# The value products of a pair of heads in one visit of the tensor engine instead of two

## The chip, the cores and the metric

The kernel runs on one core of a Trainium2 chip. The metric is the device time of one execution in microseconds (us). Engines are named as the profile names them: PE is the tensor engine (matmuls; PEld its weight loads), DVE the vector engine, ACT the scalar engine, POOL the GpSimd engine, SP the queue that issues the transfers.

## The reference

Attention with a decay, then a soft mixture of experts, then a second, dense mixture. The change touches the attention alone, which for 4 batches x 8 heads of 576 positions and 64 channels is

```python
scores = scale * np.matmul(q, k.transpose(0, 1, 3, 2))
cum = np.cumsum(log_f, axis=-1)
decay = cum[:, :, :, None] - cum[:, :, None, :]
scores = np.where(causal, -1000000000.0, scores + decay)
scores = scores - np.max(scores, axis=-1, keepdims=True)
attn = np.exp(scores)
attn = attn / (np.sum(attn, axis=-1, keepdims=True) + 1e-09)
return np.matmul(attn, v).astype(np.float32)
```

The two mixtures behind it (some 460 of the 674 us of the profile) work on its output and are the same in both kernels.

## The kernel before

The 32 heads run as 16 pairs. The 576 rows of a head are cut into row blocks j = 0 to 3 of 128 rows and j = 4 of 64 rows; being causal, block j needs keys up to its own end only. A pair takes seven steps, `STEPS`: head 0 with blocks 0 and 1 together (step 0), 3 (step 1) and 2 (step 2); block 4 of both heads at once (step 3); head 1 with blocks 0 and 1 (step 4), 3 (step 5) and 2 (step 6). I call S0 to S6 the scores of these steps and T0 to T6 their transposes.

- **Scores, `scores(g)`.** Each product is two matmuls in float32r (lines 227 and 228); step 3 is eight matmuls on line 212 into two PSUM tiles `sc`. Then `soft` runs: a DVE instruction on line 198 adds the mask and finds the row minimum while it moves the scores into the buffer `p` of that block, and ACT takes the exponential in place (line 202, followed by its read of the row sum, which gives the signal that the block is ready). There is one `p` buffer for each block number. For step 3 DVE does this in two pieces (384 and 192 columns), then ACT takes all 576 columns in one instruction, and two small DVE copies on line 219 (`rs<-r`) take the row sums from what ACT left.
- **Transposes, `transposes(g)`.** PE turns each 128x128 piece of `p` into a PSUM tile `pt` (lines 249, 251, 258; two such tiles in turn), and DVE or ACT copies it to SBUF, into `pta` (blocks 0 and 1) or `ptb` (blocks 2, 3, 4), by line 170 (DVE), 168 (ACT) or 255. They run two steps behind the scores.
- **Value products.** `av_a` (line 288) multiplies `pta` and `av_b` (line 276) `ptb` by v, for the pair before the one whose scores are running. Both heads' products go to the two halves of the partitions of one PSUM tile, with 64 columns of weights each, as two matmuls side by side. `av_b(pr, i, q0, q1)` takes key block i and query columns q0 to q1 of the 320 that `ptb` holds: columns 0 to 127 are row block 2, 128 to 255 row block 3, 256 to 319 row block 4. After i = 2 the tile is copied to `ot` by ACT and the next v is loaded (`load_v`).
- **Operands of the next pair.** `split_a` and `split_b` cast and split q and k into `opd`: for the next pair's head 0 at steps 3 and 4, which must wait until S3 has read the old one. That is a cast on ACT (line 168), one on DVE (line 170, 128x576), a copy and two subtractions on POOL (lines 180, 179 and 190).

**Order.** In the attention PE runs in the order in which the code stands (`manual_schedule` with PE alone); DVE, ACT, POOL and SP are put in order by the framework. At step st of a pair the loop issues S(st), then `before_tr`, then T(st-2), then `after_tr`. So PE's order is: S2, **visit 1**, T0, S3, **visit 2**, T1, S4, T2, S5, T3, `nat` (line 303), S6, `plog` (lines 322 and 324), T4, S0 and T5, S1 and T6, S2 of the next pair. Visit 1 holds `av_a` and three calls of `av_b`, visit 2 the other three. Every fourth pair has the batch's own work as well (`dlog`, `csoft1`, `dnat`, `sadd`).

Of the kernel before, what the change touches and what calls it, by code (L numbers as in the profile page):

```python
# [34 lines left out]
def soft_moe_kernel(tc, a, out):  # L35
# [12 lines left out]
    with ExitStack() as top:  # L48
# [117 lines left out]
        def copy(eng, o, i):  # L166
            if eng is act:
                act.copy(o, i)  # L168
            else:
                dve.tensor_copy(o, i)  # L170
# [98 lines left out]
        def av_b(pr, i, q0, q1=320):  # L269
            if i == 3:  # L270
                av[pr] = tlq.tile([128, 512], F32, tag="av", name=f"avb_{pr}")
            t = av[pr]
            kk = 64 if i == 4 else 128
            b0 = 960 if i == 4 else 320 * i + q0
            for hh in range(2):
                pe.matmul(t[64 * hh:64 * hh + 64, q0:q1], lhsT=v_raw[pr][:kk, i, 64 * hh:64 * hh + 64],  # L276
                          rhs=ptb[2 * pr + hh][:kk, b0:b0 + q1 - q0], start=i == 3, stop=i == 2, skip_group_check=True)
            if i == 2:
                copy(EV[7], ot[pr][:, 256:576], t[:, 0:320])
                if pr + 1 < B * NP:  # L280
                    load_v(pr + 1)

        def av_a(pr, i):
            if i == 0:
                av[pr] = tlq.tile([128, 512], F32, tag="av", name=f"ava_{pr}")
            t = av[pr]
            for hh in range(2):
                pe.matmul(t[64 * hh:64 * hh + 64, 128 * i:256], lhsT=v_raw[pr][:, i, 64 * hh:64 * hh + 64],  # L288
                          rhs=pta[2 * pr + hh][:, 256 * i:256 + 128 * i], start=i == 0, stop=i == 1)
            if i < 1:  # L290
                return
            ot[pr] = ot_t
            copy(EV[0], ot[pr][:, 0:256], t[:, 0:256])
            ri = sm.tile([128, 5, 2], F32, tag="ri", bufs=2, name=f"ri_{pr}")
            h0 = 2 * pr % 6
            dve.tensor_scalar(ri, rs[:, :, h0:h0 + 2], 1e-9, None, op0=ALU.add)
            dve.reciprocal(ri, ri)
            rinv[pr] = ri
# [14 lines left out]
        def nat(pr):  # L313
            b, p = divmod(pr, NP)
            if p == 0:
                xn[b] = xnp.tile([128, 5, DM], F32, tag="xn", name=f"xn_{b}")
            nat_dve(pr, nat_pe(pr))
# [83 lines left out]
        def sadd(b, between=None):  # L401
            dn = lb[b]["dn"]
            t = tlq.tile([128, 512], F32, tag="av", name=f"sa_{b}")
            for c in range(4):
                o = 32 * c
                pe.matmul(t[o:o + 32, :], lhsT=dn[:, c, :], rhs=xn[b][:, c, :], start=True, stop=False)
            if between:
                between()
            for c in range(4):
                o = 32 * c  # L410
                n = slice(128 * c, 128 * c + 128)
                pe.matmul(t[o:o + 32, n], lhsT=dn[:64, 4, :], rhs=xn[b][:64, 4, n], start=False, stop=True)
            if b == B - 1:
                return t
            dve.scalar_tensor_tensor(s_sb, s_sb, lb[b]["al"], t, op0=ALU.mult, op1=ALU.add)
# [3 lines left out]
        def logits(pr):  # L419
            b, p = divmod(pr, NP)  # L420
            plog(pr)
            if p == NP - 1:
                rep4(b)

        def before_tr(g):

            pr, st = divmod(g, NS)
            pr -= 1
            if pr < 0:
                return  # L430
            b, p = divmod(pr, NP)
            if st in (2, 3):
                if st == 2:
                    for i in range(2):
                        av_a(pr, i)

                for x in ((3, 128), (4, 256), (0, 128)) if st == 2 else ((0, 0, 128), (1, 0), (2, 0)):
                    av_b(pr, *x)
            elif st == 6 and b and p == 0:
                sadd(b - 1)  # L440
                nat(pr)
            elif st == 6 and pr < LASTP:
                logits(pr)
# [49 lines left out]
        for g in range(NG + 4):  # L493
            pr, st = divmod(g, NS)
# [29 lines left out]
            if g == NG:  # L524
                load_pair("opd1")
            before_tr(g - LAG + 2)
            if LAG <= g < NG + LAG:
                transposes(g - LAG)
# [16 lines left out]
        pr = B * NP - 1  # L545
        with tc.manual_schedule(engines={E.PE, E.Activation, E.DVE}):
# [49 lines left out]
            i4t, st, dg, one = scr[0:32, 0:128], scr[0:32, 128:130], scr[0:32, 130:162], scr[0:32, 162:290]  # L596
# [490 lines left out]
        with tc.manual_schedule(engines={E.PE, E.Activation, E.DVE, E.Pool}):  # L1087
            for m in range(NM):
# [82 lines left out]
                if e == E2 - 1:  # L1171
                    for tt in range(2):
                        i = 2 * nb + tt
# [59 lines left out]
```

## Time and profile before

| what | number |
|---|---|
| time, median of 3 runs | 677.42 us (676.77 to 678.02) |
| the profiled execution | 675.4 us, of which 673.6 us are its span |
| PE busy over the span | 657.5 us, 98% |
| DVE / ACT / POOL busy over the span | 494.5 / 341.8 / 419.0 us |
| from 100 to 140 us (attention): PE / DVE / ACT / POOL busy, of 40 us | 39.92 / 34.41 / 27.40 / 26.81 us |
| value products of line 276 | 384 matmul instructions, 43.8 us busy |

The attention runs from the start to about 212 us. Each float32 matmul of the code shows as two instructions in the trace. A matmul's row tells when it started and a modelled time until its result stands, so rows of one engine overlap; how long PE really spends on something is read from one start to the next. The span leaves out 1.8 us around it that the time has.

### The profile page before, as it was taken

The page shows a single profiled execution, that of the slowest core. Times are in us where ns is not written, and L with a number is a line of the kernel's source. Part 1 is how long each engine was busy: PE and PEld are TensorE (multiplying, and loading weights), DVE is VectorE, ACT ScalarE, POOL GpSimd, SP SyncE. Part 2 cuts the span into 40 slices and gives each one's busy share as a digit, 9 for nine tenths or more (in the row PEclk, how much of TensorE's full clock was granted, in tenths as well). Part 3 has the DMA queues.
Part 4 walks back from the last instruction along what each step waited for, and adds up shares of the span by engine and source line. Part 5 has one row for each costly group of instructions (what it writes and reads, how often), then busy time and mean ns, then how long its engine had stood idle before and what let it go on. Part 6 is the DMA issues. An engine that isn't in the chain of part 4 may idle for free.

```text
span 673.6 us, 15304 instructions
## 1 busy us (share of the span) xinstructions
PE 657.5 (98%) x5642; PEld 580.3 (86%) x5642; DVE 494.5 (73%) x1358; ACT 341.8 (51%) x817; POOL 419.0 (62%) x392
## 2 busy tenths in 40 slices
PE   5999999999999998999999999999999999999997
PEld 3877777777777446999999999999999999999997
DVE  7888988988986103976778876778876778877774
ACT  4776767767763015543446443446543356543441
POOL 5677767767751046944589844589934589935442
PEclk7999999999999999999999999999999999999999
DMA  6678788733318894033000303000303000011111
GB/s 184 189 261 254 220 279 262 229 93 117 93 55 310 334 419 165 2 126 126 1 1 2 126 1 125 2 1 2 124 3 111 15 1 1 32 37 59 48 48 63
DMA packets 27138, 76.15 MB, mean 113 GB/s; under 512 B 3772, under 2 KB 4156, under 8 KB 27064
## 3 DMA queue, kind: packets, MB, share of 16 engines
q1 hardware_dynamic: 27064, 75.18, 32.5%
q8 instruction: 45, 0.74, 0.5%
q14 instruction: 29, 0.24, 0.1%
HBM read 70.31 MB, written 4.72 MB: 111 GB/s over the span
## 4 chain that ended last, share of the span: by engine, by line
PE 91%; DVE 3%; ACT 2%; issue 2%; SPq 1%; DMA 1%; POOL 0%; ACTq 0%; DVEq 0%
PE R L1023 27%; PE Q L1023 13%; PE P L1023 6%; PE avb L276 6%; PE pt L258 5%; PE two L835 5%; PE sc L228 3%; PE d L1043 3%; PE sc L212 3%; PE sc L227 3%; PE two L731 2%; PE pl L324 2%; PE pt L249 2%; PE ava L288 2%; PE so_ps L755 2%
## 5 line engine op out<-in xcount | busy, mean ns | idle before, releaser
L901 POOL TENSOR_TENSOR s<-S,s 128x512 fp32r<-128x512 f32 x136 | 174.9, 1320 | 134.7 <-ACT s L897 134.7
L897 ACT CAST s<-S 128x512 fp32r<-128x512 f32 x136 | 75.0, 619 | 85.9 <-DVE S L893 47.9
L202 ACT ACTIVATE p<-p,nm 128x256 f32<-128x256 f32 (+2 forms) x144 | 83.4, 580 | 37.7 <-DVE nm L198 36.9
L1023 PE MATMUL R<-wh_T,s 128*128 128x256 f32 x544 | 86.6, 281 | 0.7 <-DVE acc L1006 0.7
L1006 DVE SCALAR_TENSOR_TENSOR acc<-R,dpn,acc 128x256 f32<-128x256 f32 x115 | 55.4, 482 | 37.2 <-PE R L1023 34.2
L867 ACT ACTIVATE a<-two 128x256 f32<-128x256 f32 x68 | 26.1, 384 | 96.9 <-PE two L835 90.5
L1023 PEld LDWEIGHTS R<-wh_T,s 128*128 128x128 f32 x544 | 73.4, 188 | 1.4 <-ACT a L876 1.2
L198 DVE CUSTOM_DVE_ANT_0 p<-sc,maskb 128x256 f32<-128x256 f32 (+2 forms) x144 | 66.1, 488 | 3.3 <-PE sc L212 0.9
L893 DVE SCALAR_TENSOR_TENSOR S<-two,S 128x256 f32<-128x256 f32 x136 | 57.0, 419 | 3.4 <-POOL s L901 0.8
L893 DVE SCALAR_TENSOR_TENSOR S<-two,a 128x256 f32<-128x256 f32 x136 | 56.2, 413 | 0.0
L179 POOL TENSOR_TENSOR opd<-raw,opd 64x576 fp32r<-64x576 f32 x30 | 44.6, 1487 | 11.2 <-ACT opd L168 9.8
L258 PE MATMUL pt<-ident,p 128*128 128x128 f32 x288 | 47.3, 283 | 1.8 <-DVE ptb L255 0.8
L227 PE MATMUL sc<-opd 128*128 128x256 f32 (+3 forms) x128 | 47.1, 378 | 1.6 <-ACT opd L168 1.6
L190 POOL TENSOR_TENSOR opd<-raw,opd 64x576 fp32r<-64x576 f32 x31 | 44.1, 1424 | 6.7 <-DVE opd L170 5.7
L258 PEld LDWEIGHTS pt<-ident,p 128*128 128x128 f32 x288 | 31.3, 142 | 17.6 <-issue 13.1
L835 PE MATMUL two<-c4t,gs 128*128 128x256 f32 x288 | 46.1, 283 | 0.3 <-ACT gs L168 0.3
L883 DVE SCALAR_TENSOR_TENSOR q<-two,q 128x512 fp32r<-128x512 f32 x68 | 46.2, 679 | 0.0
L1023 PE MATMUL R<-wh_T,q 128*128 128x256 f32 x272 | 43.8, 283 | 0.0
L276 PE MATMUL avb<-ptb,v 128*64 128x192 f32 (+3 forms) x384 | 43.8, 347 | 0.0
L1023 PE MATMUL Q<-wh_B,s 128*128 128x256 f32 x272 | 43.2, 281 | 0.0
L1023 PE MATMUL Q<-wh_T,s 128*128 128x256 f32 x272 | 43.1, 280 | 0.0
L1023 PE MATMUL R<-wh_B,a 128*128 128x256 f32 x272 | 43.0, 280 | 0.0
(244 smaller groups left out, 1662.5 us busy)
## 6 DMA issues: line engine op xcount, KB each, us to landing
w<-in_w SPq DMA_DIRECT2D x50, 512.0 KB, 4.9
ring<-in_m SPq DMA_DIRECT2D x28, 512.0 KB, 6.2
raw<-in_k SPq DMA_DIRECT2D x64, 144.0 KB, 2.8
v<-in_v SPq DMA_DIRECT2D x16, 320.0 KB, 4.0
out<-acc SPq DMA_DIRECT2D x18, 256.0 KB, 2.0
raw<-in_q SPq DMA_DIRECT2D x15, 288.0 KB, 4.3
ring<-in_w SPq DMA_DIRECT2D x8, 512.0 KB, 4.7
w_opd<-in_w SPq DMA_DIRECT2D x4, 512.0 KB, 6.0
```

Source lines behind the costliest of these rows:

```text
L198: dve.tensor_tensor_reduce(out=pt_in[j][:, k0:k0 + n], in0=sc, in1=maskb[:, m0:m0 + n], scale=-SCALE, scalar=nm, op0=ALU.add, op1=ALU.min, ...
L202: act.activation(p, p, AF.Exp, bias=nm, scale=-1.0, accum_out=sums)
L227: pe.matmul(o, lhsT=qa[hh][:, qs], rhs=ka[hh][:, 0:n], start=True, stop=False)
L258: pe.transpose(t[:, i, :], pt_in[j][:, 128 * i:128 * i + 128], ident)
L276: pe.matmul(t[64 * hh:64 * hh + 64, q0:q1], lhsT=v_raw[pr][:kk, i, 64 * hh:64 * hh + 64], rhs=ptb[2 * pr + hh][:kk, b0:b0 + q1 - q0], star ...
L835: pe.matmul(t[:, j, k], lhsT=gs[e][:, 128 * fc:128 * fc + 128], rhs=c4t[:, nb * BLK:nb * BLK + BLK])
L883: dve.scalar_tensor_tensor(o[:, 1], i, 0.0, f32(o[:, 0]), op0=ALU.max, op1=ALU.subtract)
L893: dve.scalar_tensor_tensor(sv[m, name][:, c], half[m, h][:, :, k, 128 * t:128 * t + 128], 0.0, other, op0=ALU.max, op1=op)
L897: act.copy(tile_of(m, name)[:, 0], sv[m, name])
L901: (eng or pool).tensor_tensor(o[:, 1], sv[m, name], f32(o[:, 0]), op=ALU.subtract)
L1006: dve.scalar_tensor_tensor(o, t, pcol, o, op0=ALU.mult, op1=ALU.add)
L1023: pe.matmul(t, lhsT=a[:, c, :], rhs=w[:, c, :], start=first and x == 0 and c == 0, stop=x == 2 and c == 3, skip_group_check=True)
```

## The change

In `before_tr` the second visit goes, and its three calls of `av_b` follow the first visit's. The call (1, 0), key block 1 with all 320 columns, is cut in two, (1, 128) and (1, 0, 128), so that everything which needs only columns from 128 on stands first, and the calls with columns 0 to 127, which need T6 of head 1, stand last.

```diff
-            if st in (2, 3):
-                if st == 2:
-                    for i in range(2):
-                        av_a(pr, i)
-
-                for x in ((3, 128), (4, 256), (0, 128)) if st == 2 else ((0, 0, 128), (1, 0), (2, 0)):
+            if st == 2:
+                for i in range(2):
+                    av_a(pr, i)
+                for x in ((3, 128), (4, 256), (0, 128), (1, 128), (0, 0, 128), (1, 0, 128), (2, 0)):
                     av_b(pr, *x)
```

PE in the kernel before, the end of visit 1 in the fourth pair, up to the beginning of visit 2 (L276 are the value products, L249 is T0, L212 is S3; in brackets what a row waits for):

```order
L276 MATMUL avb_682<-ptb_553,v_550 64x192
L276 MATMUL avb_682<-ptb_588,v_550 64x192
L249 MATMUL pt_689<-ident,p_122 128x128 [waits PE_49,Activation_49]
L249 MATMUL pt_689<-ident,p_123 128x128 x2
L212 MATMUL sc_0_695<-opd_92 128x384 [waits Pool_49]
L212 MATMUL sc_0_695<-opd_91 64x384 x2
L212 MATMUL sc_0_695<-opd_92 128x384 [waits DMAHW3_49,Pool_49]
L212 MATMUL sc_1_696<-opd_92 128x192
L212 MATMUL sc_1_696<-opd_91 64x192 x2
L212 MATMUL sc_1_696<-opd_92 128x192
L276 MATMUL avb_682<-ptb_553,v_550 64x128
L276 MATMUL avb_682<-ptb_588,v_550 64x128 [waits Activation_49]
```

The same place on PE in the changed kernel, from the new (1, 128) on:

```order
L276 MATMUL avb_686<-ptb_592,v_526 64x192
L276 MATMUL avb_686<-ptb_557,v_526 64x128
L276 MATMUL avb_686<-ptb_592,v_526 64x128 [waits Activation_49]
L276 MATMUL avb_686<-ptb_557,v_526 64x128
L276 MATMUL avb_686<-ptb_592,v_526 64x128
L276 MATMUL avb_686<-ptb_557,v_526 64x320
L276 MATMUL avb_686<-ptb_592,v_526 64x320
L249 MATMUL pt_704<-ident,p_122 128x128 [waits PE_49]
L249 MATMUL pt_704<-ident,p_123 128x128 x2
L212 MATMUL sc_0_710<-opd_92 128x384 [waits Pool_49]
L212 MATMUL sc_0_710<-opd_91 64x384 x2
L212 MATMUL sc_0_710<-opd_92 128x384 [waits DMAHW3_49,Pool_49]
```

All value products now stand ahead of T0 and S3, and T1 (line 258) follows right behind the last row of S3. S3 waits for POOL and a transfer as before.

DVE before, at the same place: the two pieces of S3 (line 198, tile `sc_0` and `sc_1`), the cast of the next pair's k between them, and what follows:

```order
L198 ISA p_126,nm_4_0_706<-sc_0_695,maskb 128x384 [waits PE_49,Activation_49]
L198 ISA nm_4_0_706 128x1
L170 CAST opd_91<-raw 128x576 [waits DMAHW1_49,DMAHW7_49,PE_49,Pool_49]
L198 ISA p_126,nm_4_1_708<-sc_1_696,maskb,nm_4_0_706 128x192 [waits DVE_49,PE_49]
L198 ISA nm_4_1_708 128x1
L219 COPY rs<-r_3_705 64x1 [waits Activation_49]
L219 COPY rs<-r_3_705 64x1
L170 COPY ptb_727<-pt_726 128x4x128 [waits PE_49]
L198 ISA p_123,nm_1_0_738<-sc_733,maskb 128x256 [waits PE_49]
```

And in the changed kernel:

```order
L198 ISA p_126,nm_4_0_721<-sc_0_710,maskb 128x384 [waits PE_49,Activation_49]
L198 ISA nm_4_0_721 128x1
L170 CAST opd_91<-raw 128x576 [waits DMAHW1_49,DMAHW2_49,PE_49,Pool_49]
L198 ISA p_126,nm_4_1_723<-sc_1_711,maskb,nm_4_0_721 128x192 [waits DVE_49,PE_49]
L198 ISA nm_4_1_723 128x1
L170 COPY ptb_733<-pt_732 128x4x128 [waits PE_49]
L198 ISA p_123,nm_1_0_744<-sc_739,maskb 128x256 [waits PE_49,Activation_49]
L198 ISA nm_1_0_744 128x1
L219 COPY rs<-r_3_720 64x1 [waits Activation_49]
L219 COPY rs<-r_3_720 64x1
```

The cast still stands between the two pieces; the copy of T1's result and the first piece of S4 have moved ahead of the two small copies that wait for ACT.

## Rows read from the trace of the kernel before

**Rows 1.** Busy time of each engine, granted clock, DMA share: a stretch of attention.
```profile
100.00:140.00 40.00, 39.92 (x331) 30.38 (x331) 34.41 (x127) 27.40 (x81) 26.81 (x31) 1.00 0.74 227
```

**Rows 2.** Timeline of PE over one pair (start us, us, what): S3 to S3.
```profile
99.82 1.31 PE L212 MATMUL sc<-opd 128*128 128x384 f32 x8
...
104.48 0.63 PE L258 MATMUL pt<-ident,p 128*128 128x128 f32 x4
...
107.66 0.28 PE L228 MATMUL sc<-opd 66*128 66x128 f32 x1
107.78 0.62 PE L258 MATMUL pt<-ident,p 128*128 128x128 f32 x4
...
108.74 0.52 PE L258 MATMUL pt<-ident,p 128*128 128x128 f32 x3
...
111.71 1.33 PE L212 MATMUL sc<-opd 128*128 128x384 f32 x8
```

**Rows 3.** Timeline of PE in short windows of the next pair: the value products.
```profile
110.13 0.28 PE L288 MATMUL ava<-pta,v 128*64 128x128 f32 x2
110.24 0.49 PE L276 MATMUL avb<-ptb,v 128*64 128x192 f32 x4
...
112.77 0.27 PE L212 MATMUL sc<-opd 66*128 66x192 f32 x1
...
112.97 0.71 PE L276 MATMUL avb<-ptb,v 128*64 128x128 f32 x6
...
113.24 0.71 PE L276 MATMUL avb<-ptb,v 128*64 128x320 f32 x4
...
114.04 0.44 PE L276 MATMUL avb<-ptb,v 128*64 128x320 f32 x2
114.41 0.33 PE L258 MATMUL pt<-ident,p 128*128 128x128 f32 x1
...
116.20 0.63 PE L258 MATMUL pt<-ident,p 128*128 128x128 f32 x4
```

**Rows 4.** Timeline of DVE, ACT and POOL behind S3 of the first pair.
```profile
100.91 0.56 DVE L198 CUSTOM_DVE_ANT_0 p<-sc,maskb 128x384 f32<-128x384 f32 x1
...
101.12 0.67 POOL L180 TENSOR_SCALAR opd<-raw 64x576 fp32r<-64x576 f32 x1 [1.12 <-PE sc L212]
...
101.39 0.71 DVE L170 CAST opd<-raw 128x576 fp32r<-128x576 f32 x1
...
102.02 0.40 DVE L198 CUSTOM_DVE_ANT_0 p<-sc,maskb,nm 128x192 f32<-128x192 f32 x1
...
103.21 0.19 ACT L202 ACTIVATION_READ_ACCUMULATOR p<-p,nm 128x1 f32 x1
...
103.43 0.31 DVE L219 COPY rs<-r 64x1 f32<-64x1 f32 x2 [1.00 <-ACT p L202]
...
103.66 0.68 DVE L170 COPY ptb<-pt 128x512 f32<-128x512 f32 x1
...
108.26 0.34 DVE L255 COPY ptb<-pt 64x64 f32<-64x64 f32 x2
```

**Rows 5.** Timeline of DVE and POOL at the same place of the next pair.
```profile
113.28 0.46 DVE L170 CAST opd<-raw 128x576 fp32r<-128x576 f32 x1
...
113.73 0.67 POOL L180 TENSOR_SCALAR opd<-raw 64x576 fp32r<-64x576 f32 x1 [1.85 <-DMA raw<-in_q]
```

**Rows 6.** Timeline near the start: PE waits for ACT alone.
```profile
14.31 0.19 ACT L202 ACTIVATION_READ_ACCUMULATOR p<-p,nm 128x1 f32 x1
...
14.55 0.47 PE L249 MATMUL pt<-ident,p 128*128 128x128 f32 x1 [0.87 <-ACT p L202]
```

**Rows 7.** Timeline of PE and ACT in a pair with the batch's own work.
```profile
74.22 0.44 PE L212 MATMUL sc<-opd 128*128 128x384 f32 x1
...
77.87 0.19 ACT L202 ACTIVATION_READ_ACCUMULATOR p<-p,nm 128x1 f32 x1
...
79.27 0.27 PE L258 MATMUL pt<-ident,p 128*128 128x128 f32 x1
```

## The prediction

> **What bounds the kernel now.** I read the busy time by stretches first. In attention PE is busy 39.92 of 40 us at the full clock, 2.4 GHz (granted 1.00), and DVE 34.41 [rows 1]. That looks like PE alone. But a matmul's busy time is modelled and covers short waits, so I then went along the timelines of PE, DVE and ACT over one pair, and asked at each transpose what had just ended.
>
> One pair lasts 11.89 us, from S3 at 99.82 to S3 at 111.71 [rows 2]. Counted from the first S3:
> - DVE's first piece of S3 starts at 1.09, the cast of the next k at 1.57, the second piece at 2.20, and ACT's exponential of block 4 is signalled at 3.58 (103.21 + 0.19) [rows 4].
> - Only then (DVE sat idle for 1.00 "<-ACT p") the two small copies run, and behind them the copy of T1's result, 103.66 to 104.34 [rows 4]. T3, which needs the PSUM tile that this copy empties, starts 0.14 later, at 104.48 [rows 2].
> - From there DVE works on until the copies of line 255 end at 108.60 [rows 4], and T6 starts 0.14 later, at 108.74 [rows 2].
>
> So the loop is tied to a chain, not to PE alone: S3 on PE, two pieces and a cast on DVE, the exponential on ACT, the small copies and T1's copy on DVE, T3 on PE. PE and DVE are nearly balanced on it. The reader should look at what stands on PE **between S3 and T3**, since that is the work that covers this chain, and visit 2 is the largest piece of it.
>
> **The change part by part.**
>
> *The visit that goes.* In the next pair S3's last matmul starts at 112.77, visit 2 at 112.97, T1 at 114.41 [rows 3]. S3's eight matmuls start over 112.77 - 111.71 = 1.06 us [rows 2, 3], which is four of 384 columns and three of 192, eleven times 192, with some 0.1 for the change from T0: about 0.09 for 192 columns. So visit 2 holds PE for 114.41 - 112.86 = 1.55 us. Of that, its columns cost: a pair of 128-column products takes 0.11 (110.13 to 110.24), a pair of 320 columns 0.27 (113.24 to 114.04 for three) [rows 3]; two and four of these are 0.22 + 1.08 = 1.30. The rest, 0.25, is switching between full-width and half-width weights: 0.11 before its first matmul, 0.05 more on its first pair (112.97 to 113.24 for two), about 0.10 before T1.
>
> *What it adds.* The 1.30 us of products reappear in visit 1. The cut of (1, 0) adds 2 matmuls a pair, 32 in all; a pair of 192 columns takes the difference of 320 and 128, 0.16, so 0.16 + 0.11 equals the uncut 0.27 and the weight loads stay hidden: I take nothing, and 0.05 a pair at most. T1 now follows S3 directly. Scores of 128 columns to a transpose take 0.12 (107.66 to 107.78) [rows 2], about 0.05 more than the scores alone: T1 starts 1.06 + 0.09 + 0.05 = 1.20 after S3, not 2.70. So PE saves 2.70 - 1.20 - 1.30 = **0.20 us a pair** (0.09 to 0.25 with the new switch taken at 0.16 or at nothing).
>
> *What the saving runs into.* From T1 to T3 PE needs 1.79 (114.41 to 116.20) [rows 3], so PE would be ready for T3 at 1.20 + 1.79 = 2.99. The chain through DVE and ACT begins with S3 and is not shortened: the cast still stands between the two pieces. The exponential is signalled at 3.58, and PE starts 0.05 behind such a signal (14.50 to 14.55) [rows 6]. So T3 starts at **3.63** and PE stands idle for 0.64. It used to have 1.55 us of visit 2 as cover here; that cover now stands ahead of S3, where nothing needs it.
>
> *What is late next.* DVE no longer waits with T1's copy for the exponential. It can start when the second piece ends, 2.60 (102.02 + 0.40) [rows 4], and the stretch from there to the end of line 255 is 108.60 - 103.66 = 4.94 plus the 0.31 of the small copies that now lie inside it: 7.85, T6 at 7.99. By PE, T6 comes 4.26 behind T3 (104.48 to 108.74) [rows 2]: 7.89. I take 7.94. From T6 to the next S3 it was 2.97 and is 4.27 with the moved products. The pair then lasts **12.20 us, 0.31 more than 11.89**.
>
> *The cast.* In the first pair POOL starts its copy of q at 101.12, ahead of DVE's cast, which takes 0.71; in the next one q lands late, POOL starts at 113.73 and the cast takes 0.46 [rows 4, 5]. With S3 moved 1.30 later while that q was asked for at the old place, POOL will be ready in every pair and the cast long. Three of the pairs have the short cast now and lose about 0.2 more each. The range takes the other end, short casts throughout.
>
> *Pairs with the batch's own work* (three). Here T3 starts 79.27 - 74.22 = 5.05 after S3 and the exponential is signalled at 3.84 [rows 7]: PE alone is the bound. Without visit 2 T3 would come at 3.55, and must wait until 3.89: +0.34 - 0.20, about 0.15 more each.
>
> *Covered, hence nothing.* The products of columns 0 to 127 wait for ACT's copy of T6's result. T6 starts at 108.74 and the first product of `ptb` at 110.24 [rows 2, 3]; the ones that wait stand three calls and now a fourth, 1.2 us, behind that, near 111.5. T6's 0.52 and a copy of at most 0.68 [rows 2, 4] end before 110, with 1.5 us left for ACT's queue. ACT's copy of the products to `ot` comes earlier than before, and in a gap of ACT. `load_v` is issued 1.5 us earlier; nothing on SP behind it waits longer. POOL's split for the next head follows S3 as before; S0, its user, comes 1.0 nearer to it (with T3 at 3.63 and not 4.66). PE's waits in this part of the trace name no POOL, so I cost that at nothing; if the reserve is gone, it works as C does.
>
> *Sum.* Between 16 groups S3 there are 15 intervals. The first holds no visit 2 and gains a longer visit 1: +1.3. Eleven ordinary ones: 11 x 0.31 = +3.4, and 3 x 0.2 = +0.6 for the casts. Three of batches: +0.45. Behind the last S3, T3 moves forward by 1.0 (4.66 to 3.63) to 1.5 (PE alone): -1.2. Together **+4.5 us**. Against the profiled execution of 675.4 that is 679.9; it lies 2.0 below the median of the runs, so in terms of the runs 677.42 + 4.5 = **681.9**.
>
> **The rivals.**
>
> *A: PE is the bound and the switches are the gain.* Visit 2's 0.20 goes, and no wait takes its place. A pair would be 1.20 + 1.79 + 4.26 + 4.27 = 11.52, 0.37 less; with 11 of these, less 0.6 for the three that are short already, 3 x 0.2 and about 0.2 at the ends, -4.3: 673.1. For it speak PE's 39.92 of 40 us and the switches that the rows show. Against it: the exponential would have to be signalled at 2.94, 0.64 earlier than it was, and no instruction of its chain was removed. Chance 0.12. The Trainium skill, page TensorEngine Tiling (Array Packing), section Key Properties, says that changing the tiling mode drains the engine; by that rule two drains a pair go and the kernel gets faster. The trace shows such a drain at both ends of visit 2 (0.16 and 0.10 us), so the rule holds here, but it counts PE alone.
>
> *B: no difference.* The cast is short in every pair, because q still lands late or POOL starts behind it. The exponential is then signalled 0.25 earlier, an ordinary pair lasts 11.95, the three short ones lose nothing extra: 0.7 + 0.45 + 0.1, about +1.2: 678.6. Against it: q's transfer hangs on the scores of the pair before, not on S3. Chance 0.13.
>
> *C: slower still.* DVE, which starts T1's copy and S4's first piece ahead of the small copies, is stopped by these for longer than I allow (they wait for the signal at 3.58, and by my count DVE is there at about 3.6, with no reserve). 0.2 us a pair more: 14 x 0.2 = 2.8, 684.7. Chance 0.12.
>
> That the change does not do what it says I leave out: the order on PE shows the one visit.
>
> **How the numbers follow.** A measurement of this kernel can tell about 0.2%, 1.35 us, from no change. My forecast has 0.63 and with C 0.75 for slower; B has 0.13 for the same; A 0.12 for faster. The unknown terms move the forecast between +1.2 (short casts) and +7.3 (C). The range from 676.6 to 684.8 holds forecast, B and C and leaves out A.
>
> **What would show it.** In the profile of the changed kernel: visit 2 gone, line 276 with 448 matmuls in place of 384; T1 some 1.2 us behind S3; PE idle before T3 for 0.5 to 0.7 us with "<-ACT p" as what ended it; casts of 0.71 in all ordinary pairs; pairs of about 12.2 us; the small copies behind S4's first piece. I am wrong if T3 follows S5 without a gap (A), or if T3's gap is there and the pairs are no longer than 11.9 us, which would mean that PE between T6 and S3 has become shorter than I count.

## The result and the profile after

The changed kernel takes **681.12 us** (median; 680.73 to 683.6) beside 677.01 us of the kernel before on the same chip (675.12 to 678.02): 1.0075 times the time by all runs together (the quotient of the two medians alone is 1.0061), 95% interval 1.0059 to 1.0091, so 4.0 to 6.2 us slower. The forecast was slower, 681.9 us. The profiled execution took 681.9 us, its span 680.1 (before: 673.6).

First the stretch of attention as in [rows 1]; PE is no longer busy all the time, 37.82 of 40 us at the full clock against 39.92:

```profile
100.00:140.00 40.00, 37.82 (x332) 29.90 (x334) 34.58 (x125) 27.27 (x79) 27.39 (x30) 1.00 0.73 236
```

What PE waited for between 20 and 200 us of the changed kernel (line, what it waited for: us in total, times, longest):

```profile
PE pt L258 <- ACT p L202: 7.3, 11, 0.8
PE pt L258 <- ACT dt L380: 2.1, 3, 0.7
PE pt L249 <- ACT p L202: 0.2, 1, 0.2
```

and the same of the kernel before:

```profile
PE pt L258 <- DVE ptb L170: 0.3, 1, 0.3
PE pt L249 <- ACT p L202: 0.2, 1, 0.2
```

Eleven waits for an exponential (line 202) and three for line 380, 9.4 us in all, are new. One ordinary pair on PE, S3 to S3, the rows that answer to [rows 2, 3]:

```profile
154.10 1.32 PE L212 MATMUL sc<-opd 128*128 128x384 f32 x8
155.25 0.60 PE L258 MATMUL pt<-ident,p 128*128 128x128 f32 x4
...
157.73 0.66 PE L258 MATMUL pt<-ident,p 128*128 128x128 f32 x4 [0.63 <-ACT p L202]
...
162.01 0.52 PE L258 MATMUL pt<-ident,p 128*128 128x128 f32 x3
...
163.51 2.53 PE L276 MATMUL avb<-ptb,v 128*64 128x192 f32 x28
166.28 0.42 PE L212 MATMUL sc<-opd 128*128 128x384 f32 x1
```

T1 follows S3 after 1.15 (it was 2.70), T3 after 3.63, T6 after 7.91, and the next S3 after 12.18. The whole visit, 28 matmuls of line 276, now stands between T6 and S3. Behind S3, DVE and ACT do this (to be read beside [rows 4]):

```profile
155.19 0.56 DVE L198 CUSTOM_DVE_ANT_0 p<-sc,maskb 128x384 f32<-128x384 f32 x1 [0.24 <-PE sc L212]
...
155.67 0.71 DVE L170 CAST opd<-raw 128x576 fp32r<-128x576 f32 x1
156.30 0.40 DVE L198 CUSTOM_DVE_ANT_0 p<-sc,maskb,nm 128x192 f32<-128x192 f32 x1
...
156.63 0.68 DVE L170 COPY ptb<-pt 128x512 f32<-128x512 f32 x1
157.24 0.41 DVE L198 CUSTOM_DVE_ANT_0 p<-sc,maskb 128x256 f32<-128x256 f32 x1
...
157.70 0.31 DVE L219 COPY rs<-r 64x1 f32<-64x1 f32 x2
```

```profile
157.49 0.19 ACT L202 ACTIVATION_READ_ACCUMULATOR p<-p,nm 128x1 f32 x1
```

Piece, cast, piece and exponential stand at the same distances from S3 as before (1.09, 1.57, 2.20, signal at 157.68, 3.58 behind S3), T1's copy runs ahead of the small copies, and PE starts T3 0.05 behind the signal. What had been covered by visit 2 is now waited for.

**Where the time is**, by the starts of S3 (an interval runs from one S3 to the next). From the first to the sixteenth: 184.69 us before, 191.99 after, +7.30. Of that +1.49 are the first interval (10.75 to 12.24), +3.13 eight ordinary ones (median 11.89 to 12.21), +0.83 the three that lead into a pair with the batch's own work, and **+1.85 the three that begin with the S3 of such a pair** (13.71 to 14.33 each; "behind" below). The stretch from the last S3 to the end of the attention is 1.15 shorter, and the first S3 came 1.26 earlier: 13.84, where the profiles of the experiments have 13.8 to 15.2 with no change there, so this is no gain of the change. Later, 1.1 us were lost in this one execution at 226 to 232 us, where the granted clock was 0.72 of full on average (0.50, the lower of the two levels, 1.2 GHz, from 228 to 230; from 212 to 226 PE had been busy for 12.8 us at full clock). Busy by stretches:

```profile
226.00:232.00 6.00, 5.43 (x58) 3.15 (x61) 0.56 (x2) 0.38 (x1) 0.56 (x2) 0.72 0.70 238
```

The same 32 matmuls took 3.0 us there (by groups of lines, after) and 1.9 before:

```profile
L729 PE MATMUL two<-ring,si_t 128*32 128x256 f32 x32 | 3.0, 536 | 0.1
```

```profile
L731 PE MATMUL two<-ring,si_t 128*32 128x256 f32 x32 | 1.9, 381 | 0.1
```

Some of the profiles below of kernels with the one visit have such a dip (e1_uncut), some have none (e5_lt0, e8b_late), and e10_more has one with both visits: it isn't part of what the change costs every execution. Whether the change makes it more frequent stays open. These parts come to 6.0 of the 6.5 us by which the span grew; the other 0.5 I did not place.

**The pair with a batch's work**, beside [rows 7]. PE waits at T2 for the exponential of the batch's logits; T3 comes 4.36 behind S3 (75.69):

```profile
78.62 0.55 PE L258 MATMUL pt<-ident,p 128*128 128x128 f32 x3 [0.71 <-ACT dt L380]
...
80.05 0.61 PE L258 MATMUL pt<-ident,p 128*128 128x128 f32 x4
```

On DVE an addition of a constant to five columns (line 361) stands between the second piece of S3 and T1's copy, and lasts 0.81 us:

```profile
78.15 0.40 DVE L198 CUSTOM_DVE_ANT_0 p<-sc,maskb,nm 128x192 f32<-128x192 f32 x1
...
78.48 0.81 DVE L361 TENSOR_SCALAR cs<-cs 128x5 f32<-128x5 f32 x1
79.20 0.68 DVE L170 COPY ptb<-pt 128x512 f32<-128x512 f32 x1
```

It ends at 79.29, just behind POOL's subtraction on line 179 (79.26):

```profile
77.77 1.49 POOL L179 TENSOR_TENSOR opd<-raw,opd 64x576 fp32r<-64x576 f32 x1
```

In the kernel before it stood 2 us behind T1's copy, which ended 4.11 behind S3 (74.22), and lasted 0.15:

```profile
77.64 0.69 DVE L170 COPY ptb<-pt 128x512 f32<-128x512 f32 x1 [0.75 <-PE pt L258]
...
80.27 0.15 DVE L361 TENSOR_SCALAR cs<-cs 128x5 f32<-128x5 f32 x1
```

### The profile page after: what moved, and what is told of

It reads as the page before. It is cut to its first block, busy times and chain, and to the rows that moved or that the text cites. A ratio compares the mean times of both kernels' runs of the same rounds, so it can differ in the third digit from the quotient of the medians.

```text
span 680.1 us, 15429 instructions
## 1 busy us (share of the span) xinstructions
PE 656.3 (97%) x5706; PEld 585.1 (86%) x5706; DVE 497.6 (73%) x1358; ACT 342.4 (50%) x817; POOL 419.2 (62%) x392
## 4 chain that ended last, share of the span: by engine, by line
PE 87%; DVE 4%; ACT 4%; issue 3%; DMA 0%; ACTq 0%; POOL 0%; DVEq 0%
PE R L1021 26%; PE Q L1021 13%; PE P L1021 6%; PE avb L276 6%; PE pt L258 5%; PE two L833 5%; PE d L1041 3%; PE sc L212 3%; PE sc L228 2%; PE two L729 2%; PE sc L227 2%; PE pl L324 2%; PE pt L249 2%; PE ava L288 2%; PE so_ps L753 2%
## 5 line engine op out<-in xcount | busy, mean ns | idle before, releaser
L180 POOL TENSOR_SCALAR opd<-raw 64x576 fp32r<-64x576 f32 x30 | 21.2, 705 | 40.9 <-PE sc L212 32.4
L1021 PE MATMUL R<-wl_T,s 128*128 128x256 f32 x272 | 43.0, 280 | 0.0
```

The lines of the kernel that those rows point to most:

```text
L1021: pe.matmul(t, lhsT=a[:, c, :], rhs=w[:, c, :], start=first and x == 0 and c == 0, stop=x == 2 and c == 3, skip_group_check=True)
```

## The experiments

Theory: the chain S3, two pieces and the cast, the exponential, T3 sets the pace, and work between S3 and T3 on PE is cover for it. Rivals: the cut or the long visit costs the time; moved work costs in proportion; PE alone is the bound. "T3 behind S3" is the median of the eleven pairs of the loop without a batch's work, "ordinary" the median of the eight ordinary intervals, "behind" the three that begin in a pair with a batch's work, all from one trace of each kernel. e4_cast_after, e4_cast_before and e8_batch leave out part of the computation and measure time alone.

| kernel | T3 behind S3 | ordinary | behind | time against before (95%) |
|---|---|---|---|---|
| before | 4.66 | 11.89 | 13.71 | 1 |
| changed | 3.65 | 12.21 | 14.33 | 1.0075 (1.0059 to 1.0091) |
| e1_uncut | 3.64 | 12.19 | 14.33 to 14.50 | 1.0101 (1.0080 to 1.0122) |
| e2_third | 4.68 | 12.24 | 13.72 | 1.0057 (1.0037 to 1.0076) |
| e3_behind | 7.02 | 12.74 | 14.2 to 15.1 | 1.0286 (1.0256 to 1.0315) |
| e4_cast_after | 3.25 | 11.84 | 15.9 to 18.7 | 1.0151 (1.0125 to 1.0176) |
| e4_cast_before | 4.43 | 11.64 | 13.72 | 0.9993 (0.9976 to 1.0010) |
| e5_lt0 | 3.65 | 12.19 | 14.33 | 1.0098 (1.0080 to 1.0115) |
| e7_pool | 3.25 | 11.81 | 14.96 | 1.0071 (1.0046 to 1.0095) |
| e8_batch | 3.65 | 12.20 | 15.0 to 16.6 | 1.0152 (1.0117 to 1.0186) |
| e8b_late | 3.64 | 12.19 | 13.89 | 1.0044 (1.0030 to 1.0058) |
| e9_both | 3.25 | 11.81 | 13.9 to 14.4 | 1.0034 (1.0010 to 1.0057) |
| e10_more | 4.96 | 11.58 | 13.56 to 16.7 | 1.0004 (0.9985 to 1.0022) |
| e12_halves | 4.94 | 11.57 | 13.56 | 0.9960 (0.9944 to 0.9976) |

**e1_uncut: is it the cut?**

```diff
-for x in ((3, 128), (4, 256), (0, 128), (1, 128), (0, 0, 128), (1, 0, 128), (2, 0)):
+for x in ((3, 128), (4, 256), (0, 128), (0, 0, 128), (1, 0), (2, 0)):
```

> The changed kernel with one edit: the products of block 1 are not cut at column 128, so two matmuls a pair fewer; the one visit stays. My theory (T3 is tied to the exponential of block 4, not to PE): whatever PE saves in this visit stands ahead of S3, so a pair gets shorter by what the cut cost, 0 to 0.05 us, and the time is that of the changed kernel, 680.4 to 681.2 us (before: 677.0). Rival (the loss comes from the cut itself: weight loads that no longer hide, or the products that need the latest transposes): the loss goes, and the time is back at 677 us or below. T3 should stand 3.6 us behind S3 in both cases, ordinary pairs at 12.15 to 12.22 us by my theory, at 11.9 by the rival.

Ordinary intervals are 0.02 shorter, T3 stands where it stood. The cut costs next to nothing; the times of the two kernels (ratios 1.0101 and 1.0075) can't be told apart. The time itself was a miss: 682.56 us beside 675.78 is 5.4 to 8.2 more (95%), where I expected 3.4 to 4.2. The trace has a dip of the clock and one ordinary interval of 13.00 (PE waits 0.9 us for a transfer of `opd`, line 228) that I had not counted on; whether they fill the difference stays open. The rival falls all the same, since the loss did not go.

**e2_third: a quarter of the products moved, both visits kept** (from the kernel before).

```diff
-for x in ((3, 128), (4, 256), (0, 128)) if st == 2 else ((0, 0, 128), (1, 0), (2, 0)):
+for x in ((3, 128), (4, 256), (0, 128), (1, 128)) if st == 2 else ((0, 0, 128), (1, 0, 128), (2, 0)):
```

> The kernel before, with only the columns from 128 on of block 1 moved from visit 2 into visit 1: 0.33 of the 1.30 us of products. Both visits stay, so no switch between weight shapes is saved, and DVE's order is that of before. My theory (T3 hangs on a chain of 4.66 us that begins with S3, PE alone would be there at 4.49): T3 stays at 4.66 though PE has less ahead of it, and the 0.33 stands between T6 and S3: an ordinary pair lasts about 12.2 us, as in the full change, 11 x 0.33 = 3.6 and 0.3 for the first interval, 680.5 to 681.5 us. Rival 1 (a loss in proportion to what is moved): a quarter of the full change's, +1 us, 678.0. Rival 2 (PE is the bound, and work that is only moved is free): 677.0, pairs of 11.9 us.

As the theory had it. PE over one pair:

```profile
100.94 1.31 PE L212 MATMUL sc<-opd 128*128 128x384 f32 x8
102.19 1.20 PE L276 MATMUL avb<-ptb,v 128*64 128x128 f32 x12
...
105.60 0.63 PE L258 MATMUL pt<-ident,p 128*128 128x128 f32 x4 [0.41 <-DVE ptb L170]
...
113.14 1.33 PE L212 MATMUL sc<-opd 128*128 128x384 f32 x8
```

T3 stays 4.66 behind S3, with a wait of 0.41 in front of it that there was not before, and the pair lasts 12.20. In time that is 678.76 us beside 675.78, 2.5 to 5.1 more (95%) where 3.5 to 4.5 were expected, and rival 1 (+1) and rival 2 (0) lie outside. A quarter of the move costs an ordinary pair all that the full change costs it. That the two agree is no law: here T1's copy still stands behind the small copies, the chain keeps its 4.66, and the 0.33 moved cost all of 0.33 (11.89 to 12.24 in the median); in the full change 1.30 are moved, but T1's copy runs ahead of the small copies, T3 comes 1.03 earlier, and 0.3 is left. Behind the batch's pairs, where PE alone was late for T3, the same move costs nothing (13.72). The casts are long in all its pairs, as in the changed kernel.

**e3_behind: the one visit behind S3** (from the kernel before; all calls at `st == 3`).

```diff
-            if st in (2, 3):
-                if st == 2:
-                    for i in range(2):
-                        av_a(pr, i)
-                for x in ((3, 128), (4, 256), (0, 128)) if st == 2 else ((0, 0, 128), (1, 0), (2, 0)):
+            if st == 3:
+                for i in range(2):
+                    av_a(pr, i)
+                for x in ((3, 128), (4, 256), (0, 128), (0, 0, 128), (1, 0), (2, 0)):
                     av_b(pr, *x)
```

> One visit as in the change, but behind S3 and ahead of T1 instead of ahead of S3, with block 1 uncut. The switches that go are the same, and all products, about 2.6 us, now cover the chain that begins with S3. My theory (what cost the time is the lost cover, not the single visit): T3 comes by PE alone at about 5.6 us behind S3, with no gap ended by ACT, and a pair lasts what PE needs, 11.5 to 11.6 us: 15 x (11.55 - 11.89) is about -5 us, 671 to 673. Rival 1 (the single visit is at fault: one long stretch of products starves DVE and ACT wherever it stands): pairs of 12.2 us, 681. Rival 2 (a new wait: T0's copy into the two buffers of pta must wait for the products of columns 0 to 255 of the pair before, which now come 2 us later, and T2 waits for the PSUM tile that this copy empties; or DVE, with T1's copy about 1 us later, is the bound to T6): T3 without gap, but one at T2 or T6 of 0.3 to 0.8 us, 676 to 684.

My number was off by 24 us; the second rival came true in its kind, a new wait with DVE late, but at T0 (4.6 us in seven waits from 60 to 180 us) and not at T2 or T6, with 3.1 us for POOL at S3 besides, and stronger. No T3 waits for ACT, but DVE starves behind the visit, here for 1.19 us:

```profile
101.73 0.69 DVE L170 COPY ptb<-pt 128x512 f32<-128x512 f32 x1 [1.19 <-PE pt L258]
```

and what it then does late, PE waits for at T0, ahead of the next S3 (a pair of its shortest kind, 12.17):

```profile
96.62 1.32 PE L212 MATMUL sc<-opd 128*128 128x384 f32 x8
...
98.58 2.53 PE L276 MATMUL avb<-ptb,v 128*64 128x192 f32 x24
101.03 0.66 PE L258 MATMUL pt<-ident,p 128*128 128x128 f32 x4
...
108.52 0.52 PE L249 MATMUL pt<-ident,p 128*128 128x128 f32 x3 [0.65 <-DVE ptb L170]
```

So "more cover is better" is wrong: T1 feeds DVE, and here DVE ran out of work ahead of it. How much cover is best was not searched; e12_halves below, with 0.33 us more of it than the kernel before, is faster.

**e4_cast_after and e4_cast_before: the chain shortened.** The same edit in both kernels:

```diff
-            copy(act if h < 2 else SE[1], ka_t[h], k)
+            c = slice(0, 64) if h > 1 and h % 2 == 0 else slice(0, S)
+            copy(act if h < 2 else SE[1], ka_t[h][:, c], k[:, c])
```

> The changed kernel; DVE's cast of k for the even heads (from the second pair on) covers 64 of its 576 columns, so that about 0.6 us of the 0.71 go from between the two pieces of S3. The other 512 columns of the rounded k are left out of the computation, so this is a test of time alone. My theory (T3 hangs on the chain S3, piece, cast, piece, exponential of block 4): the exponential is signalled at 3.0 after S3 and not 3.58, T3 starts at 3.0 to 3.05, where PE is ready by itself, and an ordinary pair lasts 11.5 to 11.65 us against 12.2: about -6 us in all, 674 to 676 on a chip where the kernel before takes 675.8. Rival (T3 is held by something else, or T6 is held by DVE's further work): T3 moves, T6 does not, pairs stay at 12.0 to 12.2.

> The kernel before with the same cut of DVE's cast of k (64 of 576 columns for the even heads; the rest is left out of the computation). My theory (with visit 2 as cover PE alone would be at T3 after 4.49, and the chain was at 4.66): the chain gets 0.6 shorter, but T3 moves only to 4.49, so a pair gains 0.17 at most where the cast was long and nothing where it was short: pairs of 11.65 to 11.75, -1 to -2 us in all. So the same cut should be worth three to four times as much in the changed kernel as here. Rival (DVE's total work is the bound in both): the same gain in both kernels, about 0.5 us a pair, -6 to -8 us here too.

S3 and T3 of an ordinary pair, first in the changed kernel with the cut, then in the kernel before with it (the edit moves the lines by one, L213 is S3, L259 T3):

```profile
157.03 1.34 PE L213 MATMUL sc<-opd 128*128 128x384 f32 x8
...
160.28 0.66 PE L259 MATMUL pt<-ident,p 128*128 128x128 f32 x4 [0.24 <-ACT p L203]
```

```profile
100.13 1.31 PE L213 MATMUL sc<-opd 128*128 128x384 f32 x8
...
104.54 0.61 PE L259 MATMUL pt<-ident,p 128*128 128x128 f32 x4
```

In the changed kernel T3 moves from 3.65 to 3.25, still 0.05 behind the exponential, and T6 with it: 11.84, a gain of 0.37, less than the 0.55 to 0.7 I expected. The second piece of S3 started 1.81 behind S3 (158.84) and not 0.6 earlier than 2.20; in e7_pool, where no cast at all stands between the pieces, it starts at 1.81 too, so the cast had held the chain by some 0.4 only. In the kernel before T3 comes at 4.43, by PE, and the pair lasts 11.64, a gain of 0.25. That T3 follows the chain in the one and stops at PE in the other is as expected; "three to four times as much" isn't: it is one and a half times, and the cut itself was smaller in the kernel before, where the cast of 64 columns lasted 0.45 in this pair (101.69 to 102.14), as long as POOL's copy beside it (to 102.10); over all 15 its mean is 0.365 there and 0.249 in the changed kernel. In time the cut kernel before can't be told from the whole one (675.71 beside 676.39; -1 to -2 us was expected). The total of the changed kernel rose to 687.03 us, where I had expected 674 to 676, because DVE's row in the batch's pairs was put in another order: the gates' work now stands between the pieces, and two of its instructions last over a microsecond, each until just after a subtraction of POOL ends (132.83 and 134.31):

```profile
131.67 1.20 DVE L362 TENSOR_SCALAR cs<-cs 128x5 f32<-128x5 f32 x1
...
133.31 1.19 DVE L364 TENSOR_TENSOR cn<-ce,cs 128x160 f32<-128x160 f32 x1
```

```profile
131.44 1.39 POOL L179 TENSOR_TENSOR opd<-raw,opd 64x576 fp32r<-64x576 f32 x1
132.91 1.40 POOL L191 TENSOR_TENSOR opd<-raw,opd 64x576 fp32r<-64x576 f32 x1
```

**e5_lt0, e8_batch and e8b_late: the batch's pairs.** e5_lt0 alone moves the logit tile:

```diff
-            t0 = ptq.tile([128, 512], F32, tag="pt", name=f"lt0_{b}")[:, 0:64]
+            t0 = tlq.tile([128, 512], F32, tag="av", name=f"lt0_{b}")[:, 0:64]
```

> The changed kernel with one edit: the logit tile t0 that the three pairs with a batch's own work write comes from the pool of the value products, not from the pool of the transposes. In the changed kernel PE waits 0.7 us at T2 in each of these pairs, for ACT's exponential that reads t0, since T2 needs this PSUM buffer. My theory (the 1.85 us that the three pairs lost, where I had 0.45, are this wait, which visit 2 used to cover): the wait goes, and 0.5 to 0.7 us in each pair come back: 679.0 to 679.7 against 681.1. Rival (T3 waits for the exponential of block 4 in these pairs as well and takes up what T2 gives): T2 earlier, T3 where it was, no change, 681.1. A third way: the first value products of the visit now wait for a buffer of their pool that t0 holds; then the wait moves there, and the time is the same or up to 1 us more.

T2's wait went, and T3 came at 4.34 instead of 4.36; the time, 682.32 us beside 675.78, shows no gain. What PE waits for now in these three pairs, and T3's row (S3 at 76.50):

```profile
PE pt L258 <- DVE cs L362: 1.6, 3, 0.5
```

```profile
80.83 0.63 PE L258 MATMUL pt<-ident,p 128*128 128x128 f32 x4 [0.53 <-DVE cs L362]
```

The profile names line 362, the instruction behind T1's copy on DVE; it is this copy (80.01 to 80.69) that T3 needs, by the order in which the PSUM tiles are used. My theory was half of it, the rival had the wrong cause.

> The changed kernel with the logit tile t0 from the pool of the value products (as in e5) and, for the first three batches, without the sum, the added constant and the reciprocal behind the exponential of the gates on DVE (left out of the computation; a plain copy stands for the division). Reason: in the changed kernel DVE does the added constant, five columns, between the second piece of S3 and T1's copy, and it lasts 0.81 us in each of the three pairs with a batch's work, until POOL's subtraction ends; in the kernel before the same instruction stood behind T1's copy and lasted 0.15. With t0 moved alone T3 stood at 4.34 after S3 and its copy of T1 had ended 0.14 before. My theory: both waits stood at about 4.35, so both have to go: T3 comes with the exponential, 3.9, and the interval is 13.9 and not 14.33: 3 x 0.45 = -1.3 us, 679.5 to 681. Rival: a third wait holds T3 at 4.3 and nothing changes.

e8_batch put `dve.tensor_copy(cn[:, b], ce)` in place of the gates' sum. It doesn't answer its question: the copy was put between the pieces of S3 and lasted 1.44 us beside POOL, and T3 came at 5.03. e8b_late keeps the work and makes it wait for the small copies, by a shared buffer (`r4` and `cs` become slices of one tag), with t0 as in e5_lt0:

```diff
-                r4 = sm.tile([128, 1], F32, tag="r4", bufs=1, name=f"r4_{pr}")
+                r4 = sm.tile([128, 5], F32, tag="r4", bufs=1, name=f"r4_{pr}")[:, 0:1]
...
-            cs = sm.tile([128, 5], F32, tag="cs", bufs=1, name=f"cs_{b}")
+            cs = sm.tile([128, 5], F32, tag="r4", bufs=1, name=f"cs_{b}")
```

> The changed kernel, complete, with t0 from the pool of the value products and the tile of the gates' sum sharing the one buffer of the row sums of block 4, so that DVE can begin that sum, the added constant and the reciprocal only behind the small copies, and so behind T1's copy. My theory (in the three pairs with a batch's work T3 was held at 4.35 by two waits at once, t0's exponential at T2 and DVE's added constant ahead of T1's copy): with both out of the way T3 comes at 3.9, 0.05 behind the exponential of block 4, and the interval lasts 13.85 to 13.95 us and not 14.33: 3 x 0.43 = -1.3 us, 679.5 to 681. Rival: T3 stays at 4.3, or T6 is held by DVE, where the gates' work now stands: 14.3, no change.

T3 at 3.87, intervals of 13.89, 679.41 us beside 675.90. On DVE T1's copy now follows the second piece, and line 361 lasts 0.20:

```profile
78.73 0.40 DVE L198 CUSTOM_DVE_ANT_0 p<-sc,maskb,nm 128x192 f32<-128x192 f32 x1
...
79.06 0.68 DVE L170 COPY ptb<-pt 128x512 f32<-128x512 f32 x1
```

```profile
81.68 0.20 DVE L361 TENSOR_SCALAR cs<-cs 128x5 f32<-128x5 f32 x1
```

So two waits, nearly equally late, held T3 in these pairs, and taking away the one that was tried alone showed nothing. Line 361 alone was not taken away; in the changed kernel T1's copy ended at 4.19, 0.14 more is 4.33, and PE by itself came at 4.36.

**e7_pool and e9_both: can the changed kernel be repaired?** The cast of k goes to POOL; e9_both adds the edits of e8b_late.

```diff
-            copy(act if h < 2 else SE[1], ka_t[h], k)
+            if h > 1 and h % 2 == 0:
+                pool.tensor_scalar(ka_t[h], k, 1.0, 1.0, op0=ALU.mult, op1=ALU.mult)
+            else:
+                copy(act if h < 2 else SE[1], ka_t[h], k)
```

> The changed kernel, complete, with the cast of k for the even heads (from the second pair on) on POOL and not on DVE. My theory: DVE's second piece of S3 follows the first, the exponential comes 0.6 earlier and T3 at about 3.0 as in the run with the cut cast, pairs of 11.6 us, 674 to 676. What speaks against it: POOL now works from 1.3 to about 6 us behind S3 on q and k of the next head, and S0, which needs them, stands at 6.45 in the changed kernel and would stand at 5.85. If POOL is late there, PE waits at S0 for what is missing: 0.2 to 0.6 us a pair, 677 to 681. If the casts on POOL also slow DVE's copies, T6 is later still.

> The changed kernel, complete, with both repairs: the cast of k for the even heads on POOL (e7) and the batch work behind T1's copy (as in e8b). In e7 ordinary pairs lasted 11.80 us, but the three intervals behind a pair with a batch's work 14.96, since the gates' work had moved between the pieces of S3. My theory: 11.80 stays, 14.96 becomes 13.5 to 13.9 (T3 at 3.5 or by PE at 3.55): 3 x 1.2 = -3.6 against e7's 681.5, so 677 to 679, about the kernel before. Rival: POOL, with cast, splits and the batch's own sums, is late for S0 in the batch pairs: 14.5 or more, 680 to 681.

In e7_pool T3 came at 3.25 and not at 3.0, for the reason given with e4_cast_after, and the three intervals behind took 14.96: 681.53 us, where my theory had 674 to 676. POOL is late for S0 hardly ever: PE waits there once in e7_pool (0.8 us, for a transfer of `opd`) and once in e9_both (0.3 us, for POOL, in the first pair). Ordinary pairs last 11.81, and T3 still waits for ACT (a row of e7_pool; its lines are moved by three, L261 is T3's 258, L205 is 202):

```profile
157.43 0.66 PE L261 MATMUL pt<-ident,p 128*128 128x128 f32 x4 [0.25 <-ACT p L205]
```

In e9_both the batch's pairs are mended as well (13.89 twice, one of 14.35): 677.96 us beside 675.90, 0.3% behind the kernel before (0.7 to 3.9 us). These two repairs do not bring the one visit level with it.

**e10_more and e12_halves: the other way.** e10_more is the kernel before with all of block 0 in visit 2:

```diff
-for x in ((3, 128), (4, 256), (0, 128)) if st == 2 else ((0, 0, 128), (1, 0), (2, 0)):
+for x in ((3, 128), (4, 256)) if st == 2 else ((0, 0), (1, 0), (2, 0)):
```

> The kernel before with the opposite of the change in a small dose: all of block 0 moves from visit 1 into visit 2 (0.33 us of products, and two matmuls a pair fewer since block 0 is no longer cut). Both visits stay. My theory (what stands between S3 and T3 covers the chain of 4.66 us, and PE was there at 4.49): PE reaches T3 at 4.82, the chain ends before that, and the 0.33 are missing between T6 and S3, so T6 comes at about 9.05 and an ordinary pair lasts 11.65 to 11.75 us where it lasted 11.9, nothing changes where it lasted 11.62, nor in the pairs with a batch's work: 8 x 0.17 is about -1.4 us, 674.5 to 675.5 beside 676.4. Rival (moved work is free, PE is the bound): pairs as before, 676.4. Rival 2 (T1 and with it DVE's copy and all of DVE's row come 0.33 later): T6 later by as much, 676.4 to 679.

The ordinary pairs got shorter than I expected, 11.58, and the time didn't move (676.28 beside 675.90): four intervals took 0.3 to 3.2 us more than the same ones of e12_halves below. In these ACT, ahead of the exponential, waited for q to land. In the longest, 16.72, the clock had its part too: PE stood idle for 1.24 us (128 to 131 us), and from 131.0 to 134.5 the granted clock was 0.51. This profile is of the slowest of the twelve executions (680.92 us; the fastest took 673.73), so the typical one loses less in this way. ACT's wait for q from 20 to 144 us:

```profile
ACT opd L168 <- DMA raw<-in_q: 11.6, 6, 3.8
```

e12_halves is e10_more, and loads each head's half of q as soon as that half has been split (`load_q` takes the rows as a new second argument; its definition is not shown):

```diff
-                        if 1 < h and h % 2 and h // 2 + 1 < B * NP:
-                            load_q(h // 2 + 1)
+                        if 1 < h and h // 2 + 1 < B * NP:
+                            load_q(h // 2 + 1, slice(64 * (h % 2), 64 * (h % 2) + 64))
```

> The kernel of e10 (all of block 0 in visit 2), complete, with q of the pair after next loaded in two halves: the rows of the even head as soon as that head is split (some 4 us earlier than the whole tile was), those of the odd head where the whole was loaded. Reason: in e10 the ordinary pairs without a disturbance lasted 11.45 to 11.68 us, but ACT waited 11.6 us in all (5.2 in the kernel before) for q to land, ahead of the exponential of block 4, and single pairs took 0.7 to 3 us more, all of them ahead of 140 us, where the weights are loaded too. My theory: with q there in time the pairs stay at 11.45 to 11.7 throughout, the intervals into and behind a batch's work at 12.7 and 13.6: about -3 us against the kernel before, 672 to 674 beside 675.9. Rival (the transfers as a whole are the limit): the wait moves to k, v or the weights, or the early half delays these, 675 to 677.

**673.83 us** beside 676.09, 0.9960 (0.9944 to 0.9976): 0.4% faster than the kernel before, and the rival falls. No wait for q is left in that view; T3 follows PE's own work, 4.96 behind S3, and the pair lasts 11.68:

```profile
97.85 1.54 PE L212 MATMUL sc<-opd 128*128 128x384 f32 x8
99.33 1.84 PE L276 MATMUL avb<-ptb,v 128*64 128x320 f32 x12
...
102.81 0.60 PE L258 MATMUL pt<-ident,p 128*128 128x128 f32 x4
...
109.53 1.52 PE L212 MATMUL sc<-opd 128*128 128x384 f32 x8
```

How much of the gain the halves alone would bring to the kernel before was not run.

## Why the prediction was right, and where it was lucky

- *The chain, not PE.* Right. T1 at 1.15 (forecast 1.20), T3 at 3.63 with a gap of 0.63 ended by ACT (3.63, 0.64), T6 at 7.91 (7.94), 4.27 from there to S3 (4.27), the ordinary intervals 12.18 to 12.22 and one of 12.37 (12.20). e2_third shows the lost cover by itself, with DVE's order and the switches as before.
- *DVE is late next.* Not shown apart from PE: in the changed kernel and in e7_pool T6 starts 0.14 to 0.15 behind line 255, as before, but in nearly all ordinary pairs of every kernel it also starts 4.2 to 4.3 behind T3. The forecast had both ends (7.99 by DVE, 7.89 by PE), and no run tells which one holds T6.
- *The casts.* 0.71 or 0.72 in eight of the eleven, 0.60, 0.79 and 0.91 in the others; none is short (0.46). The eleven ordinary intervals of the forecast cost +3.96 against 3.4 + 0.6.
- *POOL's split, costed at nothing.* Right in the changed kernel: its waits above name no POOL. The reserve is thin, though: in e1_uncut and e7_pool PE waits once each, 0.9 and 0.8 us, for the transfer of `opd` that the next head needs.
- *The ends.* The first interval cost +1.49 (forecast 1.3), the end gave back 1.15 (1.2).
- *The batch's pairs: the term that was mis-sized*, **+1.85 and not +0.45**. I took the exponential of block 4 as the only thing behind PE. Visit 2 also covered T2's wait for the logits' exponential, and T1's copy ended 4.11 behind S3 in the kernel before, later than the exponential's 3.84. With line 361 moved ahead of that copy it ended at 4.19. e8b_late, without both, has the 3.87 that I had forecast for all three (3.89).
- *The sum.* By the trace the attention, from its first S3, costs 1.49 + 3.96 + 1.85 - 1.15 = 6.15 us, not 4.5. The measured 4.0 to 6.2 holds both. Part of the closeness of 681.9 to 681.1 is therefore luck. The range held, and so did the sign.
- *Rival A*, PE as the bound, failed for the reason given: the exponential was signalled at 3.58, not 2.94. e12_halves, with the chain covered, has ordinary pairs of 11.45 to 11.76, near A's 11.52, and so is a pair of the changed kernel less its wait (12.18 - 0.63 = 11.55): A had PE's work about right and left out the wait. *Rival B* failed with its short casts. *Rival C*, DVE stopped by the small copies, didn't come in the ordinary pairs (gap of 0.05 ahead of them at most, 157.65 to 157.70); a small DVE instruction that stops T1's copy did come, another one, in the three batch pairs.

## What to carry over

Before merging two visits of an engine, find what the second one covers: go from the work behind it along the other engines, and compare the end of that chain with the engine's own arrival. Cover counts from the point where the chain ends: where the engine came later than the chain (the batch's pairs of e2_third), 0.33 us taken away cost nothing; where it came level with it, the same 0.33 cost an ordinary pair 0.35; 0.33 added took the wait away, and everything put there starved the next engine. Moving the cover can change the chain as well, so reckon both. Where a wait moves and nothing changes, look for a second one that is just as late, and look at small instructions whose order the scheduler may have changed.

## What was not expected of the hardware

- (Lines of the changed kernel.) A DVE instruction on five columns (line 361) lasted 0.15 to 0.21 us where POOL had only one-column work, and 0.81 (changed kernel, e5_lt0) and 1.20 us (e4_cast_after) beside a POOL subtraction, which ended 0.03 to 0.04 before it. A copy and a product of 128x160 took 1.44 (e8_batch) and 1.19 (e4_cast_after; 0.31 in the kernel before) in such a place. The reduction to five columns (line 360) took 0.30 to 0.33 in every place, and the reciprocal on five columns (line 362) 0.17 also inside a subtraction of POOL (changed kernel, 79.81). The Trainium skill, page SBUF — State Buffer, section Who interferes with whom, says that copies, casts and `tensor_scalar` can all take the port pair that GpSimd uses, which is an exclusive lock, under conditions on their operands, that a `tensor_tensor` with both inputs in SBUF contends with GpSimd's reads, and that `tensor_reduce` on trn2 never does. The traces agree for each of these. So what such an instruction costs here is set by where it falls more than by its size.
- The long cast of [rows 4] fits this: 576 columns take 0.46 alone [rows 5] and 0.71 where POOL's copy started first, and in e4_cast_before 64 columns take 0.45 beside that copy and 0.18 to 0.19 without it. But the long cast ends 0.31 behind the copy and not 0.04, and after a wait for all of the copy 0.46 would be expected; why stays open.
